# Staging of weight combinations in the unused triangle of P^T, and a late first layer on four accumulators, in a kernel of attention and two matrix products on one core

## The chip, the cores and the metric

The kernel runs on one core of a Trainium2 chip. The metric is the device time of one execution in microseconds (us). The engines are named as in the profile: PE is TensorE (matrix products), DVE is VectorE, ACT is ScalarE, POOL is GpSimd and SP is SyncE, whose queue issues the transfers (DMA).

## What is computed

A forgetting attention (4 batches, 8 heads, 576 positions, 64 columns each), then one layer with mish between two matrix products, then a gated layer. All is float32.

```
scores = scale * q @ k^T + (cum[:, None] - cum[None, :])      # cum: running sum of log f
attn   = softmax(where(causal, -1e9, scores))
x = (attn @ v) as 2304 x 512
h = x @ w_in                                # 512 -> 2048, the "first layer"
x = (h * tanh(softplus(h))) @ w_out         # mish, 2048 -> 512
a, b = x @ w1, x @ w2                       # 512 -> 1024 each
out = ((a * b) @ w3) @ w_out2               # 1024 -> 1024 -> 512
```

## The kernel before

A float32 product is made of three products of halves: an operand is split into hi (a cast on ACT) and lo (the raw value less hi, on DVE or POOL), and hi·hi, hi·lo and lo·hi are added up in the accumulator. The large layers are moreover made as products of 2 x 2 blocks with seven products for eight; the operands of the seven are sums of blocks, on the weights' side made once beforehand.

**Phase A** takes 85 slots with PE's order written out. It computes the attention of 16 pairs of heads. P is the softmax's numerator, which PE transposes block by block; ACT and DVE copy the blocks into `pt`, a tile with four chunks of 128 keys for each of two pairs and two heads. Since attention is causal, the chunks 2 and 3 of the columns 0 to 255 are never written. As filler between the attention's steps run the conversions of the weights, the product w3 @ w_out2 (`wp`), the first layer of batches 0 to 2 (`l1_unit`), and `build`, which makes the combinations of weights: `put` casts one into a tile `bs` (three buffers; ACT), subtracts for its lo half (POOL) and stores both to the scratch `ws` in HBM (SP), 84 times 256 KB. The sums for it are made by POOL in the one tile `bt`.

**Phase B** begins with the late first layer: batch 3, 32 units (16 rows of blocks `m`, two halves of tokens) of 12 matmuls each, in the accumulators `ps_y` and `ps_z` by turns. Each unit ends with a copy to one of three tiles `h` (ACT) and a store to the scratch `h_scr` (SP). Beside it the 16 tiles `y` of the first two batches are loaded from `h_scr` (576 KB each) and put through mish on ACT. Two quads follow, each a g layer (`k_layer` with n = 8: seven products in the order 1, 2, 6, 5, 7, 3, 4, each with eight values of f, 12 matmuls for each f), an m layer (operands T from `m_operands`) and an h layer (`k_layer` with n = 4).

`operand` makes one operand for product o and f: for product 2 it makes two sums in place in y (DVE; they are for the later products), for product 6 two others, and `halves` makes hi and lo. Operands live in a pool of 12 `x` tiles, which also holds the eight tiles X of batch 3 during the late first layer. PE's order is the program's; the other engines' orders come from a scheduler that plans by its own model, and each engine takes its instructions strictly in that order.

## Time and profile before

| what | us |
|---|---|
| median of three runs | 1038.78 |
| the three runs | 1034.14, 1038.78, 1043.15 |
| profiled execution, its own time | 1039.57 |
| its span | 1037.8 |
| TensorE busy in it | 920.5 |

The span is that of the instructions on the core, and the profiled execution's own time is 1.8 us longer. Times of the trace count from the start of the span. The granted clock is a share of TensorE's full speed, 2.4 GHz; 0.50 is 1.2 GHz. PE starts the late first layer at 470.97 and the first g layer at 537.54.

### The profile page before, as it was taken

To read this page: it belongs to the slowest core of one execution; us is meant where nothing else is said; L and a number is where in the kernel's file an instruction comes from. 1 tells how busy PE (TensorE), PEld (TensorE's weight loads), DVE (VectorE), ACT (ScalarE), POOL (GpSimd) and SP (SyncE) were. 2 spreads that over 40 slices of the span, in tenths; PEclk is the share of its full clock that TensorE was granted. 3 is DMA by queue.
4 is the path that set the end of the run, shared out by engine and by line. 5 is a ranking of instruction groups with operands and counts; after the bars stand their busy time and mean duration, and the time that the engine had idled before them with its cause. 6 is when DMAs were issued, how large, how long until landed. Compare 5 with 4: busy or idle time off the path is not lost.

```text
span 1037.8 us, 17939 instructions
## 1 busy us (share of the span) xinstructions
PE 920.5 (89%) x6432; PEld 835.9 (81%) x6432; DVE 575.5 (55%) x985; ACT 507.1 (49%) x1123; POOL 469.5 (45%) x435
## 2 busy tenths in 40 slices
PE   0589998889888999995998897999999889899998
PEld 0466667768767788884998896999999889899998
DVE  6966666654545456631038639665458833644462
ACT  1665565666656565538233444644474254422143
POOL 4633344675656640011034669645176466611053
PEclk9999999999999999998999898999999889999999
DMA  6455556787778887659724462864987435455551
GB/s 181 149 169 165 156 172 199 235 286 253 248 264 270 290 282 218 216 191 414 231 96 126 120 198 95 281 223 167 353 301 221 126 120 166 136 163 164 165 182 70
DMA packets 133071, 209.10 MB, mean 201 GB/s; under 512 B 12053, under 2 KB 66725, under 8 KB 132981
## 3 DMA queue, kind: packets, MB, share of 16 engines
q1 hardware_dynamic: 132980, 207.95, 61.6%
q8 instruction: 51, 0.84, 0.3%
q14 instruction: 40, 0.32, 0.1%
HBM read 140.86 MB, written 66.95 MB: 200 GB/s over the span
## 4 chain that ended last, share of the span: by engine, by line
PE 45%; DVE 12%; DMA 9%; issue 3%; POOL 3%; ACT 2%; SPq 1%; ACTq 0%; DVEq 0%; POOLq 0%
PE ps_x L961 9%; PE ps_x L889 8%; PE ps_y L889 5%; PE ps_z L889 5%; PE ps_z L961 4%; PE ps_l L513 4%; DMA ws<-bs 3%; DMA h_scr<-h 3%; PE ps_y L961 2%; DVE y L855 2%; PE ps_z L513 2%; PE ps_y L513 2%; DVE g_l L870 2%; DVE g_r L860 2%; DMA y<-h_scr 2%
## 5 line engine op out<-in xcount | busy, mean ns | idle before, releaser
L513 PE MATMUL ps_l<-x,wi 128*128 128x288 f32 x1152 | 171.5, 303 | 5.2 <-ACT h L517 5.1
L513 PEld LDWEIGHTS ps_l<-x,wi 128*128 128x128 f32 x1152 | 157.6, 190 | 17.0 <-ACT h L517 7.7
L870 POOL TENSOR_TENSOR g_l<-y,g_h 128x576 fp32r<-128x576 f32 x66 | 106.6, 1626 | 123.8 <-ACT g_h L868 104.3
L870 POOL TENSOR_TENSOR h_l<-ab,h_h 128x576 fp32r<-128x576 f32 x34 | 51.2, 1520 | 122.0 <-ACT h_h L868 116.5
L371 ACT ACTIVATE P<-P,sum 128x128 f32<-128x128 f32 (+2 forms) x144 | 83.1, 578 | 32.5 <-DVE sum L361 21.6
L868 ACT CAST g_h<-y 128x576 fp32r<-128x576 f32 x96 | 63.8, 673 | 66.3 <-PE ps_z L889 35.1
L889 PE MATMUL ps_x<-g_h,ws 128*128 128x288 f32 x512 | 95.5, 308 | 0.3 <-ACT o L919 0.3
L870 DVE TENSOR_TENSOR g_l<-y,g_h 128x576 fp32r<-128x576 f32 x30 | 34.3, 1143 | 102.5 <-ACT g_h L868 102.4
L889 PEld LDWEIGHTS ps_x<-g_h,ws 128*128 128x128 f32 x512 | 80.7, 200 | 0.8 <-ACT o L919 0.5
L889 PE MATMUL ps_x<-g_l,ws 128*128 128x288 f32 x256 | 59.4, 315 | 18.5 <-POOL g_l L870 14.7
L361 DVE CUSTOM_DVE_ANT_0 P<-ps_s,m 128x128 f32<-128x128 f32 (+3 forms) x128 | 56.5, 484 | 23.4 <-PE ps_s L340 22.1
L409 PE MATMUL ps_t<-ident,P 128*128 128x128 f32 x320 | 51.9, 298 | 19.5 <-ACT pt L424 10.6
L409 PEld LDWEIGHTS ps_t<-ident,P 128*128 128x128 f32 x320 | 40.1, 152 | 29.6 <-ACT P L371 13.9
L111 POOL TENSOR_TENSOR x<-xx,x 128x288 fp32r<-128x288 f32 x32 | 26.9, 862 | 81.6 <-ACT x L97 69.6
L889 PEld LDWEIGHTS ps_x<-g_l,ws 128*128 128x128 f32 x256 | 43.7, 201 | 21.3 <-POOL g_l L870 16.5
L340 PE MATMUL ps_s<-aug 64*128 64x128 f32 (+3 forms) x128 | 36.5, 554 | 23.2 <-POOL wo L111 23.1
L961 PE MATMUL ps_x<-T,gs 128*128 128x288 f32 x384 | 54.7, 297 | 2.2 <-DVE C L976 1.4
L340 PE MATMUL ps_s<-raw 64*128 64x128 f32 (+3 forms) x256 | 49.9, 470 | 6.3 <-DMA raw<-in_qk_dram 5.7
L788 POOL TENSOR_TENSOR bs<-bt,bs 128x256 fp32r<-128x256 f32 x48 | 39.1, 815 | 35.6 <-ACT bs L787 35.4
L961 PE MATMUL ps_x<-T,ws 128*128 128x288 f32 x384 | 54.2, 296 | 0.8 <-DVE C L976 0.8
L961 PEld LDWEIGHTS ps_x<-T,gs 128*128 128x128 f32 x384 | 52.2, 189 | 3.1 <-DVE C L976 1.9
L517 ACT COPY h<-ps_l 128x288 f32<-128x288 f32 x96 | 37.4, 392 | 32.7 <-PE ps_l L513 18.2
(211 smaller groups left out, 2255.6 us busy)
## 6 DMA issues: line engine op xcount, KB each, us to landing
ws<-ws SPq DMA_DIRECT2D x112, 512.0 KB
ws<-bs SPq DMA_DIRECT2D x84, 256.0 KB
h_scr<-h SPq DMA_DIRECT2D x128, 144.0 KB
y<-h_scr SPq DMA_DIRECT2D x32, 576.0 KB
ws<-gs SPq DMA_DIRECT2D x56, 256.0 KB
raw<-in_qk_dram SPq DMA_DIRECT2D x32, 288.0 KB
cvrt<-in_w3t_dram SPq DMA_DIRECT2D x16, 512.0 KB
cvri<-in_w_in_dram SPq DMA_DIRECT2D x16, 512.0 KB
```

What stands on the lines that cost most here:

```text
L111: ins = self.nc.gpsimd.tensor_tensor(lo[..., c], raw[..., c], f32(hi[..., c]), ALU.subtract)
L340: mm(ps[:, 512 * hh:512 * hh + n], t[r, q0:q0 + 128], t[r, 0:n], start=first, stop=not first)
L361: ttr(P[hh][:, :n], ps[:, 512 * hh:512 * hh + n], self.m1[:, 512 - n:], -0.125, 3.0e38, ALU.add, ALU.min, st[hh])
L371: ins = nc.scalar.activation(t[:, :n], t[:, :n], AF.Exp, bias=b, scale=-1.0, accum_out=self.sums[:, i:i + 1])
L409: tr(self.ps_t[hh][:, o + 128 * k:o + 128 * k + 128], P[:, 128 * k:128 * k + 128], self.ident)
L513: mm(o[:, :TB], w, x, start=i == 0, stop=i == 11)
L517: self.nc.scalar.copy(t, o[:, :TB])
L788: pool.tensor_tensor(st[:, 256:], x, f32(st[:, :256]), ALU.subtract)
L868: self.nc.scalar.copy(hi, raw)
L870: eng.tensor_tensor(lo, raw, f32(hi), ALU.subtract)
L889: mm(ps[:, r, :TB], w[:, 256 * a + 128 * e:256 * a + 128 * e + 128], ops[i][b][:, r], start=o in (1, 5, 2) and f == 0 and (a, b) == (0, 0) ...
L961: mm(bank[:, r, :TB], w[:, 256 * a + 128 * k:256 * a + 128 * k + 128], T[o, k][:, b, r], start=o in (1, 2, 5) and (k, a, b) == (0, 0, 0), ...
```

## The change

Three things are changed. `put` numbers its calls, and four of seven go into the unused triangle of `pt` (in place g of 0 to 3), the other three into `bs`. The late first layer takes four accumulators in turn, its copies are made by DVE, and its units come in the order of halves: all 16 blocks m of half 0, then those of half 1. In the k layers the operands are made four steps ahead where it was three, the two sums of product 2 stand behind `halves`, and the lo part is DVE's for each odd k (k is the number of the step in its layer) where it was DVE's for each third; the same rule goes for the T tiles.

```diff
@@ -60,7 +60,7 @@
 ORDER_K = (1, 2, 6, 5, 7, 3, 4)
 ORDER_M = (1, 5, 6, 2, 3, 7, 4)
 AHEAD = 7
-T_AHEAD = 3
+T_AHEAD = 4
 
 
 def f32(ap):
@@ -88,6 +88,7 @@
         self.V = {}
         self.filler = deque()
         self.nl1 = 0
+        self.late_l1 = False
         self.pe = None
 
 
@@ -158,7 +159,7 @@
 
     def l1_bank(self):
         self.nl1 += 1
-        return self.ps_l[self.nl1 % 2]
+        return self.ps_l[self.nl1 % len(self.ps_l)]
 
 
     def pools(self):
@@ -514,7 +515,10 @@
             if i == 11:
                 t = self.base.tile([128, TB], F32, name=f"h{b}_{m}_{half}", tag="h", bufs=HB)
                 with self.tc.high_priority(offset=HP_L1):
-                    self.nc.scalar.copy(t, o[:, :TB])
+                    if self.late_l1:
+                        self.nc.vector.tensor_copy(t, o[:, :TB])
+                    else:
+                        self.nc.scalar.copy(t, o[:, :TB])
                 self.nc.sync.dma_start(self.h_scr[128 * m:128 * m + 128, b * S + TB * half:b * S + TB * half + TB], t)
 
         i = 0
@@ -565,6 +569,7 @@
     def phase_a(self):
         nc = self.nc
         self.X, self.wo2t, self.w3s, self.wi, self.parts = {}, [], {}, {}, {}
+        self.nbs = 0
         self.att_pool()
 
         first = []
@@ -717,7 +722,8 @@
         self.late = ctx.enter_context(tc.tile_pool(name="late", bufs=1))
         p = ctx.enter_context(tc.tile_pool(name="psb", bufs=1, space=PSUM))
         self.banks = [p.tile([128, 1024], F32, name=n) for n in ("ps_x0", "ps_x1", "ps_y", "ps_z")]
-        self.ps_l = [t[:, :512] for t in self.banks[2:]]
+        self.ps_l = [t[:, :512] for t in (self.banks[2], self.banks[3], self.banks[0], self.banks[1])]
+        self.late_l1 = True
         self.bk = [t.rearrange("p (r w) -> p r w", r=2) for t in self.banks]
         self.wq, self.wcur = deque(), deque()
         self.wsrc = deque((l, t) for q in range(2) for l, n in enumerate((28, 28, 14)) for t in range(n) if q or l != 1)
@@ -783,10 +789,16 @@
         a11, a12, a21, a22 = self.quarters_of(l, *r)
 
         def put(o, x):
-            st = self.att.tile([128, 512], F32R, name=f"bs{l}_{u}_{o}", tag="bs", bufs=3)
-            nc.scalar.copy(st[:, :256], x)
-            pool.tensor_tensor(st[:, 256:], x, f32(st[:, :256]), ALU.subtract)
-            nc.sync.dma_start(self.ws[l][self.place(l, u, o)], f32(st))
+            self.nbs += 1
+            g = self.nbs % 7
+            if g < 4:
+                st = self.pt[:, g, 2:4, 0:256].bitcast(F32R)
+            else:
+                st = self.att.tile([128, 512], F32R, name=f"bs{l}_{u}_{o}", tag="bs", bufs=3)
+                st = st.rearrange("p (h w) -> p h w", h=2)
+            nc.scalar.copy(st[:, 0], x)
+            pool.tensor_tensor(st[:, 1], x, f32(st[:, 0]), ALU.subtract)
+            nc.sync.dma_start(self.ws[l][self.place(l, u, o)].rearrange("p (h w) -> p h w", h=2), f32(st))
 
         if k == 0:
             put(1, a11)
@@ -851,9 +863,6 @@
         b11, b12, b21, b22 = b
         tt = self.nc.vector.tensor_tensor
         hi, lo = [self.x_tile(f"{name}_{x}").rearrange("p (r w) -> p r w", r=2) for x in "hl"]
-        if o == 2:
-            tt(b11, b12, b11, ALU.subtract)
-            tt(b12, b22, b12, ALU.subtract)
         raw = {1: b11, 2: b21, 3: b22, 4: b21, 5: b11, 7: b12}.get(o)
         if o == 6:
             raw = self.x_tile(f"{name}_r", F32).rearrange("p (r w) -> p r w", r=2)
@@ -862,11 +871,14 @@
             tt(b21, b21, raw, ALU.subtract)
             return hi, lo
         self.halves(raw, hi, lo, k)
+        if o == 2:
+            tt(b11, b12, b11, ALU.subtract)
+            tt(b12, b22, b12, ALU.subtract)
         return hi, lo
 
     def halves(self, raw, hi, lo, k):
         self.nc.scalar.copy(hi, raw)
-        eng = self.nc.vector if k % 3 == 2 else self.nc.gpsimd
+        eng = self.nc.vector if k % 2 else self.nc.gpsimd
         eng.tensor_tensor(lo, raw, f32(hi), ALU.subtract)
 
     def k_layer(self, name, n, src, c, hook):
@@ -985,7 +997,7 @@
     def phase_b(self):
         self.late_pool()
         self.y = {}
-        l1 = list(self.filler) + [x for m in range(16) for half in range(2) for x in self.l1_unit(B - 1, m, half)]
+        l1 = list(self.filler) + [x for half in range(2) for m in range(16) for x in self.l1_unit(B - 1, m, half)]
         self.gate = {}
         n = -(-len(l1) // 192) * 12
 
```

The orders show where the scheduler has put this. In ACT's order before, in the late first layer, the copies of the units (h_m_half) stand among the mishes (the ACTIVATEs on y):

```order
L517 COPY h_1_0_4857<-ps_z 128x288
L842 ACTIVATE y_7_5041<-y_7_5041 128x1152
L842 ACTIVATE y_8_5074<-y_8_5074 128x1152
L842 ACTIVATE y_9_5107<-y_9_5107 128x1152
L842 ACTIVATE y_10_5140<-y_10_5140 128x1152
L842 ACTIVATE y_11_5173<-y_11_5173 128x1152
L842 ACTIVATE y_12_5206<-y_12_5206 128x1152
L842 ACTIVATE y_13_5239<-y_13_5239 128x1152
L517 COPY h_1_1_4872<-ps_y 128x288
L842 ACTIVATE y_14_5272<-y_14_5272 128x1152
L842 ACTIVATE y_15_5305<-y_15_5305 128x1152
L517 COPY h_2_0_4890<-ps_z 128x288
```

After, ACT has only mishes there, and DVE has the copies. In its order halfway through the late first layer, the lo part of g_1_3 (product 1, f = 3) and four sums on y stand between the copies of the first units of half 1:

```order
L519 COPY h_15_0_5022<-ps_y 128x288
L882 TENSOR_TENSOR g_1_3_l<-y_3_4861,g_1_3_h 128x576
L875 TENSOR_TENSOR y_2_4828<-y_2_4828 128x2x288
L875 TENSOR_TENSOR y_3_4861<-y_3_4861 128x2x288
L519 COPY h_0_1_5040<-ps_z 128x288
L876 TENSOR_TENSOR y_2_4828<-y_10_5092,y_2_4828 128x2x288
L876 TENSOR_TENSOR y_3_4861<-y_11_5125,y_3_4861 128x2x288
L519 COPY h_1_1_5055<-ps_x_4756 128x288
L519 COPY h_2_1_5073<-ps_x_4757 128x288
```

So these five operations are ahead of the g layer now, and the copies of units 16 (h_0_1) and 17 wait behind some of them. The second place is the end of product 1 in the second g layer, DVE's order before (names are layer g, product, f, and h, l or r for hi, lo and raw):

```order
L855 TENSOR_TENSOR y_3_6978<-y_3_6978 128x2x288
L870 TENSOR_TENSOR g_1_5_l<-y_5_7544,g_1_5_h 128x576
L856 TENSOR_TENSOR y_3_6978<-y_11_7677,y_3_6978 128x2x288
L855 TENSOR_TENSOR y_4_7522<-y_4_7522 128x2x288
L855 TENSOR_TENSOR y_5_7544<-y_5_7544 128x2x288
L856 TENSOR_TENSOR y_4_7522<-y_12_7698,y_4_7522 128x2x288
L856 TENSOR_TENSOR y_5_7544<-y_13_7717,y_5_7544 128x2x288
L855 TENSOR_TENSOR y_6_7582<-y_6_7582 128x2x288
L855 TENSOR_TENSOR y_7_7592<-y_7_7592 128x2x288
L870 TENSOR_TENSOR g_2_0_l<-y_8_7616,g_2_0_h 128x576
L856 TENSOR_TENSOR y_6_7582<-y_14_7752,y_6_7582 128x2x288
L856 TENSOR_TENSOR y_7_7592<-y_15_7759,y_7_7592 128x2x288
```

There g_2_0_l stands as the last but two. And after, from the sums on y_6 on:

```order
L875 TENSOR_TENSOR y_6_7541<-y_6_7541 128x2x288
L882 TENSOR_TENSOR g_1_7_l<-y_7_7551,g_1_7_h 128x576
L876 TENSOR_TENSOR y_6_7541<-y_14_7708,y_6_7541 128x2x288
L875 TENSOR_TENSOR y_7_7551<-y_7_7551 128x2x288
L882 TENSOR_TENSOR g_2_1_l<-y_9_7591,g_2_1_h 128x576
L876 TENSOR_TENSOR y_7_7551<-y_15_7715,y_7_7551 128x2x288
L882 TENSOR_TENSOR g_2_3_l<-y_11_7633,g_2_3_h 128x576
L882 TENSOR_TENSOR g_2_5_l<-y_13_7673,g_2_5_h 128x576
L882 TENSOR_TENSOR g_2_7_l<-y_15_7715,g_2_7_h 128x576
```

The first lo of product 2 that DVE makes was that of f = 0 behind all but two of the sums; now it is that of f = 1, and those of f = 0, 2, 4 and 6 are POOL's.

## Rows read from the trace of the kernel before

**Rows 1.** The page, part 1, TensorE: busy time, share of the span, instructions.
```profile
PE 920.5 (89%) x6432; PEld 835.9 (81%) x6432; DVE 575.5 (55%) x985; ACT 507.1 (49%) x1123; POOL 469.5 (45%) x435
```

**Rows 2.** Windows: width, busy us by engine (instructions), clock, DMA share, GB/s.
```profile
186.00:386.00 200.00, 177.43 (x1245) 147.37 (x1244) 107.47 (x261) 120.77 (x363) 127.92 (x159) 0.95 0.82 269
537.00:569.00 32.00, 28.29 (x202) 28.05 (x201) 28.29 (x26) 11.88 (x20) 18.27 (x11) 0.95 0.41 125
569.00:589.00 20.00, 16.23 (x101) 15.50 (x100) 16.53 (x14) 8.47 (x14) 14.47 (x9) 0.85 0.36 105
627.00:652.00 25.00, 17.41 (x104) 16.03 (x103) 23.48 (x16) 12.23 (x21) 25.00 (x15) 0.80 0.31 107
784.00:822.00 38.00, 33.91 (x237) 33.45 (x236) 33.60 (x31) 14.66 (x23) 21.02 (x13) 0.91 0.56 164
879.00:898.00 19.00, 15.44 (x106) 15.20 (x105) 15.23 (x13) 9.00 (x15) 15.70 (x9) 0.91 0.39 128
```

**Rows 3.** Waits by line in 185 to 385: in total, times, longest.
```profile
POOL bs L788 <- ACT bs L787: 51.9, 48, 3.3
ACT bs L787 <- DMA ws<-bs: 29.9, 29, 3.6
...
ACT bs L787 <- POOL bt L795: 5.4, 5, 1.7
```

**Rows 4.** Timeline of ScalarE: start, length; idle before and its releaser.
```profile
271.49 0.40 ACT L787 CAST bs<-cvu 128x256 fp32r<-128x256 f32 x1 [3.60 <-DMA ws<-bs]
```

**Rows 5.** Timeline of TensorE in the staging, the same columns.
```profile
272.55 1.54 PE L409 MATMUL ps_t<-ident,P 128*128 128x128 f32 x6 [2.47 <-ACT P L371]
```

**Rows 6.** Timeline of TensorE, late first layer.
```profile
470.97 1.88 PE L513 MATMUL ps_z<-x,wi 128*128 128x288 f32 x12 [2.00 <-ACT h L517]
...
490.17 3.25 PE L513 MATMUL ps_y<-x,wi 128*128 128x288 f32 x12 [8.64 <-ACT h L517]
...
535.95 1.75 PE L513 MATMUL ps_y<-x,wi 128*128 128x288 f32 x12
537.54 0.42 PE L889 MATMUL ps_x<-g_h,ws 128*128 128x288 f32 x2
```

**Rows 7.** Timeline of ScalarE, late first layer.
```profile
479.22 0.38 ACT L517 COPY h<-ps_z 128x288 f32<-128x288 f32 x1
...
489.74 0.38 ACT L517 COPY h<-ps_y 128x288 f32<-128x288 f32 x1
...
493.60 0.40 ACT L517 COPY h<-ps_z 128x288 f32<-128x288 f32 x1 [0.60 <-DMA h_scr<-h]
```

**Rows 8.** Timeline of SyncE's queue, late first layer.
```profile
478.62 0.32 SPq L518 DMA_DIRECT2D h_scr<-h  x1
```

**Rows 9.** A window of the late first layer, columns as in rows 2.
```profile
484.00:488.00 4.00, 0.00 (x0) 0.00 (x0) 0.66 (x1) 3.47 (x3) 0.00 (x0) 0.50 1.02 413
```

**Rows 10.** Timeline of TensorE, stops at products 2, 4 and 2.
```profile
554.46 0.53 PE L889 MATMUL ps_y<-g_l,ws 128*128 128x288 f32 x2 [3.71 <-DVE g_l L870]
...
647.33 0.85 PE L889 MATMUL ps_x<-g_l,ws 128*128 128x288 f32 x2 [3.64 <-POOL g_l L870]
...
806.75 0.85 PE L889 MATMUL ps_y<-g_l,ws 128*128 128x288 f32 x2 [3.80 <-DVE g_l L870]
```

**Rows 11.** Timeline of VectorE, beside product 1 of both g layers.
```profile
548.58 0.74 DVE L856 TENSOR_TENSOR y<-y,y 128x576 f32<-128x576 f32 x1
549.25 0.74 DVE L855 TENSOR_TENSOR y<-y 128x576 f32<-128x576 f32 x1
...
784.19 1.97 DVE L855 TENSOR_TENSOR y<-y 128x576 f32<-128x576 f32 x1 [0.45 <-POOL g_l L870]
...
804.75 1.95 DVE L870 TENSOR_TENSOR g_l<-y,g_h 128x576 fp32r<-128x576 f32 x1
```

**Rows 12.** Timeline of GpSimd in the first g layer.
```profile
536.50 7.72 POOL L870 TENSOR_TENSOR g_l<-y,g_h 128x576 fp32r<-128x576 f32 x4 [61.37 <-ACT g_h L868]
...
595.81 1.44 POOL L870 TENSOR_TENSOR g_l<-y,g_h 128x576 fp32r<-128x576 f32 x1 [1.77 <-ACT g_h L868]
```

## The prediction

> **What bounds the kernel now.** I read the page first, then the kernel in windows, then in the lossy windows the gaps of TensorE and the queue that ends each. TensorE is busy for 920.5 us, 89% of the span [rows 1], so only what it does not lose can be won: idle time, and time at a low clock. I count the loss of a stretch as idle plus busy × (1 − granted clock). Each row of [rows 2] gives one: 200 − 177.4 + 177.4 × 0.05 = 31.4 us in the staging stretch of phase A (186 to 386); 3.7 + 1.4 = 5.1 in products 1 and 2 of the first g layer (537 to 569), 4.1 + 3.1 = 7.1 in those of the second (784 to 822); 3.8 + 2.4 = 6.2 in product 6 (569 to 589); 7.6 + 3.5 = 11.1 in the last product, 4, of the first g layer (627 to 652) and 3.6 + 1.4 = 5.0 in that of the second (879 to 898). The late first layer is the other one. Its last unit takes 537.54 − 535.95 = 1.59, so 32 units need 50.9; they take 537.54 − 470.97 = 66.6 [rows 6], a loss of 15.7. The change aims at all of these and at no other place, so the sum is made of them.
>
> **1. Staging in P^T.** What now stands last: ACT's cast into a `bs` tile waited 29 times, 29.9 us in all, for the store of the tile's former content, and POOL's subtraction 51.9 us for ACT's cast; 5.4 us more of ACT are for POOL's `bt` [rows 3]. ACT takes its work in order, so what is queued behind the cast waits too: at 271.49 a cast came after 3.60 us of waiting for a store [rows 4]; the exponentials of P stood behind it, and TensorE, which transposes P, was idle for 2.47 us until 272.55 [rows 5]. Seven places instead of three let seven combinations be under way; the wait for a store then begins only when the seventh before it has not landed. Price: the same casts, subtractions and bytes, since the places in P^T are ones that the causal triangle never fills. What may eat it: a store now has 1 KB pieces where it had 2 KB, and the DMA engines are at a share of 0.82 there [rows 2]; and `bt` is one tile, so POOL's chain through it stays. The bounds: nothing, if the stores are limited by what the DMA engines move; and 18, which is the gaps of TensorE that I can follow to a store (about 10 of the 22.6 idle us) and all but one of the 8.9 us of clock. I take 8, nearer the lower end, since the next wait in the same queue (POOL's `bt`, ACT's other casts) is right behind. **−8 (0 to −18).**
>
> **2. The late first layer.** What it removes: ACT's copy of a finished unit stood among the 16 mishes, each of which waits for its load of y. After the copy at 479.22 the next ran at 489.74 with seven mishes between, and a later one at 493.60 waited for a store of h [rows 7]. TensorE had two accumulators, stood still for 8.64 us until 490.17 [rows 6], and was granted 0.50, which is 1.2 GHz, in 484 to 488 [rows 9]. Now VectorE copies, which has little else there, and four accumulators are in turn. But the copy writes one of three h buffers, and these are freed by stores. The DMA engines are full until the y loads are through (share 1.02 in [rows 9]). The first of those stores was issued at 478.62 [rows 8] and had let nobody go by 488. With it one place earlier in SP's queue I let it land near 487. So three units are copied, four more fill the accumulators, and the eighth unit starts at about 487.9 where now the sixth starts at 490.17. From there 25 units × 1.59 = 39.7 give 527.6; the next store holds the ninth for some 3 us, and the half clock after the stop costs some 2.5: 533.3 instead of 537.54. **−4.2.** Bounds: 0, if the stores land as before and the two units gained before the stop are lost at it in waits for stores; −8, if the stop is short enough for the clock not to fall. The first gap of 2.00 at 470.97 [rows 6] stays: the banks are those of phase A and its last copy is ACT's.
>
> What else moves there: with the units in the order of halves the four X tiles of half 0 are free halfway, so g_1_2, g_1_3 and the y sums of f = 2 and 3 are done beside it. They stand in VectorE's queue before h_0_1's copy, and wait for ACT's and POOL's part: at most some 4.5 us (a cast, a subtraction of 1.9, five operations of 0.7). Four accumulators last 4 × 1.59 = 6.4, so TensorE doesn't feel it. The loads of ws also go later, behind units 16 to 23, and still end some 15 us before product 1.
>
> **3. Products 1 and 2 of a g layer.** VectorE makes 16 sums for later products and a part of the lo's; the lo's of product 2 stood behind all of it. TensorE's stops in front of product 2, 3.71 and 3.80 us, end with VectorE's g_l [rows 10]. What an operation costs there depends on POOL: VectorE's 128x576 takes 0.74 alone, one every 0.67 (548.58, 549.25), and 1.95 beside POOL [rows 11]; POOL's takes 1.44 alone, and four beside VectorE took 7.72, or 1.93 each [rows 12]. So a pair takes 1.93; VectorE's share of it is its pitch of 0.67, POOL's the rest, 1.26. The check: from 784.19 to 806.70 VectorE did 17 operations [rows 11], and POOL about 9 in the same time: 17 × 0.67 + 9 × 1.26 = 22.7, measured 22.5. Now the first lo of product 2 on VectorE is the 20th operation there, with 5 to 6 of POOL beside it (half the lo's where it had two thirds): 20 × 0.67 + 5.5 × 1.26 = 20.3, so it ends at 804.2 from 783.9. Product 1 ends as before at 802.5, f = 0 of product 2 (POOL's) takes 1.6, f = 1 is wanted at 804.2 too: **−6.5 of the 7.1** in the second g layer. In the first, 10 operations are left there at the end of the late first layer, with 4 of POOL's: 6.7 + 5.0 = 11.7 to 13.5, and wanted after 12.8 + 1.6 = 14.4: the stop goes with its clock, **−5.1**. Operands four steps ahead change little by themselves: ACT's casts already run ahead as far as the x buffers let them.
>
> **4. Products 6 and 4.** Product 6 has two VectorE sums and a lo for each f, and three of the lo's were VectorE's: 19 × 0.67 + 5 × 1.26 = 19.0, which is what it took (8 × 1.6 = 12.8 and the 6.2 of loss). Now four are: 20 × 0.67 + 4 × 1.26 = 18.4, so −0.6, and some of the first lies a step earlier beside product 2: **−1 each, −2** (0 to −6). At product 4 POOL is the last: it worked 25.00 of 25.00 us [rows 2], with T's and gate pieces, and TensorE waited 3.64 us for its g_l [rows 10]. Two of its eight lo's and two T's go to VectorE, but VectorE was itself busy 23.5 of 25: **−2** in the first g layer (−1 to −4) and **−0.5** in the second.
>
> **Sum.** 8 + 4.2 + 6.5 + 5.1 + 2 + 2.5 = 28.3. The profiled execution is 1039.57 us, 0.8 above the median of 1038.78: 1039.6 − 28.3 = **1011 us**, the median likewise 1010.5.
>
> **The rivals.**
> (a) The h buffers, not the accumulators, hold the late first layer: stores land as late as now, and the units gained are given back: 1011 + 4 = 1015. For it: the copy at 493.60 waited for a store [rows 7]. Chance 0.10.
> (b) VectorE and POOL don't overlap at all: an operation holds the other for its whole length, so 20 × 0.74 + 5.5 × 1.44 = 22.7, product 2 of the second g layer waits 2.4 us again and its clock falls: 1011 + 6.5 = 1017.5. Against it: a pair measured 1.93, not 0.74 + 1.44 = 2.18, and 17 × 0.74 + 9 × 1.44 = 25.5 where 22.5 were measured. Chance 0.10. The Trainium skill's page "SBUF — State Buffer", section "SBUF: two separate sides", says this: the pair of ports that VectorE and GpSimd share is an exclusive lock, held for the whole instruction, and the loser blocks fully. By that rule the second g layer would gain next to nothing here; the trace agrees that the two hold each other up, and not in the amount.
> (c) The staging brings nothing, since the stores or `bt` take the place of the freed tile: 1011 + 8 = 1019. For it: POOL waits more for ACT's cast than ACT for stores, and the DMA share is 0.82. Chance 0.14.
> (d) More goes than I count: with four steps ahead the small stops of products 6 and 4 vanish and their low clock with them (6 + 4 more): about 1001. Chance 0.08.
> (e) The other side: VectorE becomes the bound. If an operation of VectorE costs 1.9 whenever POOL has any work, and POOL has work as long as before, then the four lo's more of VectorE in products 2, 6 and 4 add 4 × 1.9 = 7.6 a layer, 15 in two, and the 16 of parts 3 and 4 are not won: 1011 + 16 + 15 = 1042, or about 1050 where the clock falls at these stops as it does now (0.80 in [rows 2]). It decides where POOL's shorter share doesn't shorten the time that VectorE spends beside it. Against it: VectorE at 0.74 alone is half of POOL's 1.44, so work moved to it makes the sum of both smaller. Chance 0.05.
> (f) The change doesn't do what it says: the places in P^T wait for the readers of P^T and the operands stand a step ahead only in name, and the time is 1035 to 1040. Chance 0.03.
>
> **How the numbers follow.** The forecast, 1011, has 0.50. Rivals (a), (b) and (c) lie within 8 us of it and exclude one another not at all; all three together would be 1030. The range goes from (d)'s 1001, with part 1's upper bound of 10 more weighed in at less than half, to the three together: 997 to 1029. A change of under 1% (1028.4 to 1049.2) can hardly be told from none, as the three runs before differ by 0.9%. Faster by more than that: 0.50 + 0.10 + 0.10 + 0.14 + 0.08, less 0.06 for combinations: 0.86. Same: 0.10, the combinations, (f) and a part of (e). Slower: 0.04.
>
> **What would show it.** Part 1: waits of ACT's staging casts for stores well under 30 us, idle time of TensorE in 186 to 386 at 15 or less, and the late first layer starting some 8 us earlier. Part 2: one stop of 4 to 6 us in it, later, ended by VectorE's copy that waits for a store of h; 62 us instead of 66.6. Part 3: no stop over 1 us at product 2, clock 1.00 through it. Part 4: the same stops in product 6, a little shorter. I am wrong if the stops in front of product 2 are still there, if the waits for stores only turn into waits for `bt`, or if VectorE's operations take 1.9 all through.

## The result, and the profile after

The changed kernel takes 1002.0 us (median of four executions, 1000.61 to 1007.84), the kernel before 1036.63 in the same comparison; the ratio is 0.967 with an interval of 0.961 to 0.973. That is 34.6 us less, where 28 were forecast. The profiled execution of the changed kernel is the fastest of its four (1000.61, span 998.8); that of the kernel before (1039.57) was a further one, longer than three of the four that the median is from. So the two profiles stand 39.0 apart, 4 more than the medians. I account for these 39.0, by the starts of the stages in TensorE's timeline. The first stage ends where the last four matmuls of the first pair's attention with v (those on `vb`) begin, 2.6 us after the first of them; the experiments call this moment the first product of attention with v.

| stage | before | after | change | forecast |
|---|---|---|---|---|
| start to the end of the first product of attention with v | 79.98 | 77.14 | −2.8 | 0 |
| from there to the end of phase A | 390.99 | 383.27 | −7.7 | −8 |
| late first layer | 66.57 | 60.42 | −6.2 | −4.2 |
| first g layer, products 1 and 2 | 31.05 | 25.59 | −5.5 | −5.1 |
| second g layer, products 1 and 2 | 32.35 | 27.19 | −5.2 | −6.5 |
| product 6 and product 5 behind it, both g layers | 65.47 | 62.56 | −2.9 | −2 |
| product 4, first g layer | 24.24 | 19.44 | −4.8 | −2 |
| product 4, second g layer | 17.90 | 14.42 | −3.5 | −0.5 |
| all else up to TensorE's end (m layers, h layers, products 7 and 3) | 325.45 | 325.01 | −0.4 | 0 |

The page's first part, TensorE's row, answers to [rows 1]:

```profile
PE 900.3 (90%) x6432; PEld 818.9 (82%) x6432; DVE 608.5 (61%) x1051; ACT 492.3 (49%) x1091; POOL 412.6 (41%) x401
```

TensorE has 20 us less of busy time with the same instructions, since it ran less at a low clock; the rest of the 39 was idle time. The windows of the same stages, as in [rows 2], with product 6 of both g layers:

```profile
176.00:376.00 200.00, 178.81 (x1299) 149.29 (x1298) 114.04 (x277) 124.91 (x380) 130.15 (x161) 0.98 0.87 276
520.80:553.00 32.20, 32.20 (x244) 32.20 (x243) 29.04 (x31) 13.03 (x20) 15.15 (x10) 1.00 0.50 159
546.00:567.00 21.00, 17.34 (x124) 16.31 (x123) 19.24 (x18) 9.86 (x16) 11.71 (x8) 1.00 0.41 130
602.00:622.00 20.00, 15.25 (x102) 14.79 (x101) 19.93 (x18) 10.04 (x18) 15.93 (x10) 0.91 0.32 104
759.00:787.00 28.00, 26.55 (x201) 26.08 (x200) 26.97 (x29) 11.91 (x19) 13.56 (x8) 1.00 0.62 182
787.00:806.00 19.00, 14.88 (x96) 13.86 (x95) 17.84 (x17) 7.08 (x12) 9.84 (x6) 0.91 0.36 113
844.00:859.00 15.00, 13.54 (x102) 13.31 (x101) 13.61 (x14) 7.92 (x14) 9.15 (x6) 1.00 0.44 153
```

By the same count (idle plus busy × (1 − clock)) the staging loses 21.2 + 3.6 = 24.8 us of 200 where it lost 31.4. Products 1 and 2 of the first g layer lose nothing, with the clock at 1.00 all through; those of the second lose 1.5 (7.1 before). Product 6 loses 3.7 in the first (546 to 567; 6.2 before), product 4 there 6.1 (11.1 before) and 1.5 in the second (844 to 859; 5.0 before). In product 4 of the first g layer GpSimd is busy for 15.9 of 20 us and no longer all the time; VectorE is now, 19.9 of 20.

The whole staging stretch, from the end of the first row of the table to the end of phase A, before and after (the same columns):

```profile
79.98:470.97 390.99, 356.77 (x2493) 291.49 (x2487) 220.70 (x548) 230.12 (x667) 176.83 (x214) 0.97 0.73 232
77.14:460.41 383.27, 349.68 (x2494) 286.65 (x2488) 221.19 (x548) 227.89 (x667) 176.80 (x214) 0.99 0.76 237
```

TensorE's idle time hardly fell, from 34.2 to 33.6 us; the gain is in its busy time, 7.1 us less for the same products at a higher granted clock. In the window of 200 us the idle time is 21.2 after 22.6, where the prediction had named 15 or less as a sign.

The waits of the staging, by line (in total, times, longest), answer to [rows 3]; the staging casts into P^T are named `pt`:

```profile
POOL pt L800 <- ACT pt L799: 34.9, 21, 5.3
...
POOL bs L800 <- ACT bs L799: 10.4, 18, 1.7
...
ACT bs L799 <- POOL bt L813: 8.3, 8, 2.1
...
ACT pt L799 <- POOL bt L807: 6.3, 3, 3.3
...
ACT bs L799 <- POOL bt L811: 6.1, 5, 1.6
ACT pt L799 <- POOL bt L805: 6.0, 4, 1.8
...
ACT pt L799 <- DMA ws<-pt: 0.9, 1, 0.9
```

The waits of the casts for stores, 29.9 us before, are down to 0.9. GpSimd waits for the casts for 45 us in sum where it waited 52. The casts' waits for `bt` grew: 26.7 us in these four lines, where the four of the kernel before have 15.9 (5.4, 5.1, 2.9 and 2.5). So of the 29 us won at the stores some 11 came back as waits for `bt`. TensorE's longest stop left in the staging ends with an exponential that had waited for VectorE, and not for a store:

```profile
328.91 0.77 ACT L372 ACTIVATE P<-P,sum 128x576 f32<-128x576 f32 x1 [0.91 <-DVE sum L369]
...
329.83 0.66 PE L414 MATMUL ps_t<-ident,P 128*128 128x128 f32 x4 [2.93 <-ACT P L372]
```

TensorE's timeline in the late first layer answers to [rows 6]:

```profile
460.41 2.82 PE L514 MATMUL ps_z<-x,wi 128*128 128x288 f32 x12 [2.34 <-ACT h L521]
...
469.96 3.34 PE L514 MATMUL ps_x<-x,wi 128*128 128x288 f32 x24
478.09 3.25 PE L514 MATMUL ps_y<-x,wi 128*128 128x288 f32 x12 [4.79 <-DVE h L519]
482.62 1.88 PE L514 MATMUL ps_z<-x,wi 128*128 128x288 f32 x12 [1.28 <-DVE h L519]
...
520.83 0.43 PE L901 MATMUL ps_x<-g_h,ws 128*128 128x288 f32 x2
```

Seven units run before the stop: one at 460.41, two at 463.02, one each at 466.79 and 468.38, and the two at 469.96. The eighth waits 4.79 us, the ninth 1.28. VectorE's timeline says what for (these are the copies, with the idle time before and its releaser):

```profile
467.69 0.46 DVE L519 COPY h<-ps_x 128x288 f32<-128x288 f32 x1 [1.82 <-DMA h_scr<-h]
...
477.57 0.46 DVE L519 COPY h<-ps_y 128x288 f32<-128x288 f32 x1 [3.85 <-DMA h_scr<-h]
482.10 0.46 DVE L519 COPY h<-ps_z 128x288 f32<-128x288 f32 x1 [4.07 <-DMA h_scr<-h]
```

Each of the three copies waited for a store of h out of the buffer that it writes. The windows of 4 us, as in [rows 9], show that the clock fell after the stop, and for one window only (another low one, 0.71 at 462 to 466, lies behind the layer's first gap of 2.34):

```profile
474.00:478.00 4.00, 0.00 (x0) 0.00 (x0) 0.42 (x1) 3.26 (x3) 0.00 (x0) 1.00 1.04 422
478.00:482.00 4.00, 3.25 (x12) 2.90 (x12) 0.03 (x1) 2.96 (x4) 0.00 (x0) 0.57 0.78 302
482.00:486.00 4.00, 3.38 (x25) 3.38 (x26) 2.16 (x5) 0.76 (x1) 0.00 (x0) 1.00 0.37 131
```

The stops that are left in the g layers, in TensorE's timeline, answer to [rows 10]. The first two lie in product 6 and the third in product 4 of the first g layer, the last in product 1 of the second:

```profile
559.32 0.53 PE L901 MATMUL ps_x<-g_l,ws 128*128 128x288 f32 x2 [1.41 <-POOL g_l L882]
...
561.82 0.53 PE L901 MATMUL ps_x<-g_l,ws 128*128 128x288 f32 x2 [1.44 <-DVE g_l L882]
...
618.28 0.85 PE L901 MATMUL ps_x<-g_l,ws 128*128 128x288 f32 x2 [3.70 <-DVE g_l L882]
...
772.06 0.53 PE L901 MATMUL ps_x<-g_l,ws 128*128 128x288 f32 x2 [1.21 <-DVE g_l L882]
```

### The profile page after: what moved, and what is told of

It is laid out like the page before. It is cut to its first block, busy times and chain, and to the rows that moved or that the text cites. A ratio compares the mean times of both kernels' runs of the same rounds, so it can differ in the third digit from the quotient of the medians.

```text
span 998.8 us, 17936 instructions
## 1 busy us (share of the span) xinstructions
PE 900.3 (90%) x6432; PEld 818.9 (82%) x6432; DVE 608.5 (61%) x1051; ACT 492.3 (49%) x1091; POOL 412.6 (41%) x401
## 4 chain that ended last, share of the span: by engine, by line
PE 59%; DVE 16%; DMA 11%; ACT 6%; issue 4%; POOL 3%; SPq 1%; ACTq 0%; DVEq 0%; POOLq 0%
PE ps_x L901 11%; PE ps_x L973 10%; PE ps_l L514 8%; PE ps_z L901 5%; PE ps_y L901 5%; PE ps_z L973 5%; PE ps_s L443 3%; PE ps_y L973 2%; ACT P L372 2%; PE ps_s L341 2%; DMA cvru<-in_w_out_dram 2%; PE ps_x L514 2%; DMA cvri<-in_w_in_dram 2%; PE ps_t L410 2%; DMA y<-h_scr 2%
## 5 line engine op out<-in xcount | busy, mean ns | idle before, releaser
L882 POOL TENSOR_TENSOR g_l<-y,g_h 128x576 fp32r<-128x576 f32 x48 | 74.3, 1552 | 130.5 <-PE ps_y L514 56.7
L901 PE MATMUL ps_x<-g_h,ws 128*128 128x288 f32 x512 | 93.2, 301 | 2.9 <-ACT g_h L880 2.6
L882 POOL TENSOR_TENSOR h_l<-ab,h_h 128x576 fp32r<-128x576 f32 x24 | 35.5, 1480 | 126.1 <-ACT h_h L880 115.1
L901 PEld LDWEIGHTS ps_x<-g_h,ws 128*128 128x128 f32 x512 | 77.7, 193 | 4.0 <-ACT g_h L880 3.3
L882 DVE TENSOR_TENSOR g_l<-y,g_h 128x576 fp32r<-128x576 f32 x48 | 53.7, 1121 | 44.7 <-ACT g_h L880 44.1
L901 PE MATMUL ps_x<-g_l,ws 128*128 128x288 f32 x256 | 56.8, 304 | 11.1 <-DVE g_l L882 8.3
L410 PE MATMUL ps_t<-ident,P 128*128 128x128 f32 x320 | 46.7, 280 | 10.3 <-ACT pt L425 6.6
L973 PEld LDWEIGHTS ps_x<-T,ws 128*128 128x128 f32 x384 | 52.1, 189 | 2.9 <-ACT x L931 1.7
L521 ACT COPY h<-ps_l 128x288 f32<-128x288 f32 x96 | 37.5, 390 | 33.2 <-PE ps_l L514 17.3
L410 PEld LDWEIGHTS ps_t<-ident,P 128*128 128x128 f32 x320 | 37.0, 142 | 18.7 <-ACT pt L425 9.7
```

The lines of the kernel that those rows point to most:

```text
L410: tr(self.ps_t[hh][:, o + 128 * k:o + 128 * k + 128], P[:, 128 * k:128 * k + 128], self.ident)
L521: self.nc.scalar.copy(t, o[:, :TB])
L882: eng.tensor_tensor(lo, raw, f32(hi), ALU.subtract)
L901: mm(ps[:, r, :TB], w[:, 256 * a + 128 * e:256 * a + 128 * e + 128], ops[i][b][:, r], start=o in (1, 5, 2) and f == 0 and (a, b) == (0, 0) ...
L973: mm(bank[:, r, :TB], w[:, 256 * a + 128 * k:256 * a + 128 * k + 128], T[o, k][:, b, r], start=o in (1, 2, 5) and (k, a, b) == (0, 0, 0), ...
```

## The experiments

Stage times are read as in the table above, from one trace of each kernel. "Staging" is the stretch in the table's second row. Kernels 5, 6, 8, 9 and 10 were executed once, so that their medians are single times without an interval. The spread between traces is to be kept in mind: the late first layer of the change took 60.4 to 62.6 us in the six kernels that have its edits as they are (changed, 2, 5, 6, 7, 10), and the staging of the change 379.9 to 387.8 in ten.

| kernel | staging | late first layer | g1st: 1+2 | 6 | 4 | g2nd: 1+2 | 6 | 4 | median us |
|---|---|---|---|---|---|---|---|---|---|
| before | 391.0 | 66.6 | 31.1 | 19.2 | 24.2 | 32.4 | 19.0 | 17.9 | 1036.6 |
| changed | 383.3 | 60.4 | 25.6 | 17.6 | 19.4 | 27.2 | 19.4 | 14.4 | 1002.0 |
| 1 staging alone | 384.1 | 68.2 | 31.1 | 18.9 | 24.2 | 31.7 | 19.0 | 17.9 | 1028.7 |
| 2 late first layer alone | 393.3 | 62.6 | 25.6 | 18.9 | 24.1 | 31.7 | 17.1 | 17.4 | 1023.6 |
| 3 operands alone | 392.8 | 66.9 | 26.9 | 19.3 | 19.6 | 27.6 | 19.1 | 14.4 | 1019.0 |
| 4 four h buffers | 387.8 | 58.4 | 25.6 | 19.4 | 19.9 | 27.6 | 17.6 | 14.4 | 1001.9 |
| 5 third lo | 381.7 | 62.0 | 25.6 | 17.2 | 21.8 | 31.7 | 17.1 | 14.4 | 1010.2 |
| 6 three ahead | 385.7 | 61.7 | 25.6 | 17.6 | 21.5 | 27.6 | 19.4 | 15.1 | 1007.6 |
| 7 all lo on VectorE | 386.1 | 62.1 | 25.6 | 14.5 | 16.9 | 26.1 | 14.5 | 12.8 | 994.7 |
| 8 copies by ScalarE | 383.3 | 61.2 | 25.6 | 18.9 | 19.5 | 27.2 | 19.4 | 14.4 | 1004.5 |
| 9 two accumulators | 382.8 | 65.2 | 25.6 | 19.4 | 19.9 | 27.5 | 17.6 | 14.4 | 1006.0 |
| 10 four places | 390.7 | 62.4 | 25.6 | 17.6 | 19.9 | 27.6 | 19.4 | 14.4 | 1014.0 |
| 11 = 4 and 7 | 379.9 | 58.6 | 25.6 | 14.5 | 17.1 | 26.1 | 14.5 | 12.8 | 989.3 |
| 12 = 11, T shared | 383.4 | 58.0 | 25.6 | 15.0 | 16.3 | 26.1 | 15.0 | 14.0 | 990.7 |

**My theory** was that the change is three independent ones, each in its own stage, with the prices of the prediction. The rivals were its (a) to (e). The first three runs take the parts one by one.

**1. The staging alone.** Only `put` and its counter are taken from the change:

```diff
+            self.nbs += 1
+            g = self.nbs % 7
+            if g < 4:
+                st = self.pt[:, g, 2:4, 0:256].bitcast(F32R)
...
```

> Only the first part of the change: four of seven staging places in the unused triangle of P^T. My theory (the three parts act in separate stages and add up): phase A ends 8 us earlier (462 to 464 instead of 470.97, less or more by what the start of the execution differs), with the waits of the staging casts for stores under 10 us; the late first layer stays at 66 to 67 us and the g layers at 113.8 and 108.4; 1029 us. Rival (the staging brings nothing, the gain at the end of phase A comes from elsewhere): phase A ends at 469 to 472, 1037 us.

Phase A ended at 462.60, and the time is 1028.7 (ratio 0.992, 0.989 to 0.995). The casts' waits for stores, two lines of the waits:

```profile
ACT pt L794 <- DMA ws<-pt: 1.0, 1, 1.0
...
ACT bs L794 <- DMA ws<-pt: 0.4, 1, 0.4
```

1.4 us together. The late first layer took 68.2, and the g layers moved by 0.6 at most. The theory holds in time, and rival (c), that the staging brings nothing, falls.

**2. The late first layer alone.** Four accumulators, copies by VectorE, the order of halves:

```diff
...
-        self.ps_l = [t[:, :512] for t in self.banks[2:]]
+        self.ps_l = [t[:, :512] for t in (self.banks[2], self.banks[3], self.banks[0], self.banks[1])]
...
-        l1 = list(self.filler) + [x for m in range(16) for half in range(2) for x in self.l1_unit(B - 1, m, half)]
+        l1 = list(self.filler) + [x for half in range(2) for m in range(16) for x in self.l1_unit(B - 1, m, half)]
```

> Only the second part: late first layer on four accumulators, copies by VectorE, units in the order of halves. My theory: phase A as before (470 to 472), the late first layer 60 to 61 us instead of 66.6, the first g layer shorter by up to 2 (the operations that are done beside the late first layer), the second g layer at 108.4 as before; 1030 us. Rival (the h buffers hold the layer and the gain of 6 us needs the earlier y loads of the other parts): 65 to 67 us, 1036 us.

62.6 us for the late first layer, between theory and rival but nearer the theory; 1023.6 (0.988, 0.983 to 0.993). TensorE's start of it and its stop:

```profile
471.32 1.88 PE L514 MATMUL ps_z<-x,wi 128*128 128x288 f32 x12 [2.15 <-ACT h L521]
...
489.13 3.25 PE L514 MATMUL ps_y<-x,wi 128*128 128x288 f32 x12 [6.41 <-DVE h L519]
```

What I did not expect: the stop at product 2 of the first g layer is gone, all 5.5 us, with none of the third part. VectorE does a lo and four sums more during the late first layer there, and GpSimd a lo, which the order of halves allows; I take them for the reason.

**3. The operands alone.**

```diff
-T_AHEAD = 3
+T_AHEAD = 4
-        eng = self.nc.vector if k % 3 == 2 else self.nc.gpsimd
+        eng = self.nc.vector if k % 2 else self.nc.gpsimd
```

and the two sums of product 2 behind `halves`.

> Only the third part: operands four steps ahead, the sums of product 2 behind the halves, every second lo on VectorE. My theory: phase A and the late first layer as before; second g layer 99 to 100 us instead of 108.4, of which the stop at product 2 is 5 to 6.5 and product 4 3 to 4; the first g layer 103 to 106 instead of 113.8, since it starts without the operations that the second part lets run beside the late first layer; 1020 us. Rival (VectorE and GpSimd exclude each other wholly, and the first g layer's gain comes from the second part alone): the first g layer at 109 or more.

1019.0 (0.985, 0.981 to 0.990): the first g layer 104.2, the second 99.5, both in the theory's bounds and not at the rival's 109. Products 1 and 2 of the first g layer went from 31.1 to 26.9 by this part alone. The three parts alone gained 7.5, 12.6 and 17.3 us, 37.3 in sum, and together 34.6. By the stages, parts 2 and 3 remove the same stop there (4.2 us are counted twice); the medians by themselves are too wide to show it.

**4. Four h buffers** in the changed kernel (`HB = 3` becomes `HB = 4`).

> The changed kernel with four h buffers where it has three. My theory (behind the accumulators the h buffers hold the late first layer: VectorE's copies wait for stores of h): the stops of 4.79 and 1.28 us in the late first layer shrink by one unit's worth, and it takes 57 to 59 us instead of 60.4; nothing else moves; 999 us. Rival (the y loads fill the DMA engines, and the store lands when it lands; a fourth buffer only moves the stop by one unit): still 60 to 61.

58.4 us for the late first layer, so the h buffers do hold it behind the accumulators. The stops are smaller, and the longer one is still a copy that waits for a store:

```profile
480.68 1.85 PE L514 MATMUL ps_z<-x,wi 128*128 128x288 f32 x12 [0.88 <-DVE h L519]
485.30 2.04 PE L514 MATMUL ps_x<-x,wi 128*128 128x288 f32 x8 [2.77 <-DVE h L519]
```

The median, 1001.9 (0.964, 0.960 to 0.969), can't be told from the changed kernel's, and the 999 of the expectation were not reached: 2 us are lost in the spread, the staging took 387.8 here and product 6 of the first g layer 19.4.

**5. Every third lo on VectorE**, as before, in the changed kernel (`k % 2` becomes `k % 3 == 2`).

> The changed kernel with the lo of each third step on VectorE as before, and all else of the change. My theory (product 4 was won by the moved lo's of g and T, since GpSimd was full there): product 4 goes back to 22 to 24 us in the first g layer and 16 to 18 in the second; product 2 of the second g layer keeps 12.8, or loses up to 2 again. Rival (the fourth step ahead won product 4): it stays at 19.4 and 14.4.

Product 2 of the second g layer stopped again for the full 3.79 us:

```profile
782.81 0.77 PE L901 MATMUL ps_y<-g_l,ws 128*128 128x288 f32 x2 [3.79 <-DVE g_l L882]
```

so the stop there is removed by the moved lo's: the rest of the change, which this kernel has, leaves it whole. I had expected 2 us at most. Product 4 of the first g layer gave back 2.4 of 4.8 (21.8, just under the theory's bounds), that of the second nothing: its 14.4 is the rival's number.

**6. Operands three steps ahead** in the changed kernel (`T_AHEAD = 3`).

> The changed kernel with operands three steps ahead. My theory (the casts run ahead as far as the buffers let them anyway): all products within 0.7 us of the changed kernel, product 4 at 19.4 and 14.4. Rival (the step ahead won product 4 or product 2): one of them loses 3 us or more again.

Product 4 of the first g layer gave back 2.1 of 4.8, that of the second 0.7. So my sentence that the step ahead changes little by itself was wrong for product 4: there it is about as much as the moved lo's.

**7. Every lo on VectorE**, in the changed kernel:

```diff
-        eng = self.nc.vector if k % 2 else self.nc.gpsimd
+        eng = self.nc.vector
```

> The changed kernel with every lo on VectorE, none on GpSimd. My theory (beside a GpSimd operation VectorE loses 1.26 us, an operation of its own costs 0.67): product 6 takes 24 x 0.67 = 16.1 us in both g layers instead of 17.6 and 19.4, products 1 and 2 together (16 sums and 16 lo's, 21.4 us) show no stop, product 4 gets shorter since GpSimd has only the gate pieces: 17 to 19 and 13 to 14; 995 to 997 us. Rival (VectorE becomes the bound, an operation costs 1.9 as long as GpSimd has any work): product 6 at 19 or more, new stops in products 1 and 2, 1010 us.

994.7 us (0.958, 0.954 to 0.963), a little better than expected. Product 6 takes 14.5 in both layers, product 4 takes 16.9 and 12.8, and products 1 and 2 of the second g layer 26.1. VectorE's timeline in product 6 shows its three operations for each f, none stretched:

```profile
558.94 0.76 DVE L882 TENSOR_TENSOR g_l<-g_r,g_h 128x576 fp32r<-128x576 f32 x1
559.62 0.75 DVE L869 TENSOR_TENSOR g_r<-y,y 128x576 f32<-128x576 f32 x1
560.40 0.76 DVE L871 TENSOR_TENSOR y<-y,g_r 128x576 f32<-128x576 f32 x1
561.18 0.76 DVE L882 TENSOR_TENSOR g_l<-g_r,g_h 128x576 fp32r<-128x576 f32 x1
```

This decides against rival (e): VectorE has more to do and is done sooner, since what it does is not stretched to 1.9 any more. GpSimd's help there was worth less than what it cost VectorE. A part was given back: the first m layer took 95.3 us here and 92.6 in the changed kernel.

**8. Copies by ScalarE** into the four accumulators.

```diff
-                    if self.late_l1:
-                        self.nc.vector.tensor_copy(t, o[:, :TB])
-                    else:
-                        self.nc.scalar.copy(t, o[:, :TB])
+                    self.nc.scalar.copy(t, o[:, :TB])
```

> The changed kernel with the copies of the late first layer on ScalarE, as before, into the same four accumulators and in the order of halves. My theory (the stop ends with a store of h whichever engine copies; the accumulators and not the engine gave the 6 us): 60 to 62 us for the late first layer. Rival (the copies have to leave the mishes' queue): 64 to 67.

61.2 us, with one stop of 8.30 in place of two:

```profile
481.74 1.57 PE L513 MATMUL ps_y<-x,wi 128*128 128x288 f32 x5 [8.30 <-ACT h L517]
```

ScalarE's timeline has this copy behind a mish that waited for its load, and not waiting for a store:

```profile
480.24 1.16 ACT L849 ACTIVATE y<-y 128x1152 f32<-128x1152 f32 x1 [0.22 <-DMA y<-h_scr]
481.31 0.38 ACT L517 COPY h<-ps_y 128x288 f32<-128x288 f32 x1
```

So the mishes' queue held the copy longer than the h buffers did, and the units behind it then found buffers free. The time is in my bounds, but my reason, that a store ends the stop whichever engine copies, did not hold here. Against the changed kernel that is 0.8 us, within the 60.4 to 62.6 of the stage: no gain by VectorE's copying shows.

**9. Two accumulators**, with copies by VectorE.

```diff
-        self.ps_l = [t[:, :512] for t in (self.banks[2], self.banks[3], self.banks[0], self.banks[1])]
+        self.ps_l = [t[:, :512] for t in self.banks[2:]]
```

> The changed kernel with two accumulators in the late first layer, copies on VectorE. My theory (three h buffers and two accumulators hold five units where four accumulators hold seven): the stop comes two units earlier and is 3 us longer, 63 to 65 us for the late first layer. Rival (the copy by VectorE alone gave the gain): 60 to 61.

65.2 us. The stop came after five units and was longer:

```profile
476.83 3.25 PE L514 MATMUL ps_y<-x,wi 128*128 128x288 f32 x12 [6.72 <-DVE h L519]
```

So of the 6.2 us the accumulators are worth 4.7 by these two traces, and 2.6 by the longest trace with four.

**10. Four staging places**, all in P^T (`self.nbs % 4` for `self.nbs % 7`).

> The changed kernel with four staging places, all in P^T, instead of seven: 1 KB pieces in every store. My theory (the number of places counts, the 1 KB pieces cost nothing that TensorE sees): between the kernel before and the changed one, the stretch from the first product of attention with v to the end of phase A 385 to 389 us (391.0 before, 383.3 changed), waits of the casts for stores 10 to 25 us. Rival (stores in 1 KB pieces are slower and hold the staging): 391 or more, waits over 30 us.

390.7 us in the staging stretch, as the kernel before; the waits of the staging:

```profile
POOL pt L800 <- ACT pt L799: 52.0, 48, 4.0
...
ACT pt L799 <- DMA ws<-pt: 22.4, 17, 2.4
```

My number was missed, though the 22.4 us of waits for stores are in its bounds: one place more gave nothing (against 391.0 to 393.3 in the three kernels with the old staging). Whether that is the number of places or the 1 KB pieces, which here are in every store, this run doesn't separate. What it shows is that four places with 1 KB pieces are about as fast as three with 2 KB. That the step from four places to seven is what pays is likely, since pieces of 1 KB are in four of seven stores there, but not shown.

**11. The fourth h buffer and every lo on VectorE.**

> The changed kernel with every lo on VectorE and four h buffers. My theory (the two act in separate stages): late first layer 58 to 60 us, product 6 at 14.5, product 4 at 17 and 12.8 as with every lo on VectorE alone; 990 to 994 us. Rival (without GpSimd's part VectorE's queue is late in the late first layer, and the fourth buffer's gain is lost there): 62 us for it, 994 to 997 us.

989.3 us (0.954, 0.950 to 0.957), just under the expected 990 to 994: the fastest kernel here, 1.3% below the changed one, with both stages as in the single runs.

**12. The same, but the lo's of T by turns on VectorE and GpSimd.**

> The kernel with every lo of the g and h layers on VectorE and four h buffers, but the lo's of T shared by turns between VectorE and GpSimd, as in the changed kernel. My theory (an operation of GpSimd costs VectorE 1.26 where VectorE is the last, and a full T on VectorE held the m layer of the first quad at 93.7): product 4 of the first g layer 16 to 18.5, the first m layer 92 to 92.8; 988 us, within 2 of the kernel with all on VectorE. Rival (GpSimd's T operations slow VectorE's sums in product 4 as its lo's did): product 4 of the first g layer back at 19 or more, 991 us.

990.7 us (0.955, 0.952 to 0.958), not to be told from run 11. Product 4 of the first g layer is 16.3, shorter than with all on VectorE, which speaks against the rival; but the m layer behind it took 96.6 where I expected 92 to 92.8 (93.7 in run 11), and product 4 of the second g layer 14.0. So the second half of my expectation is refuted. The trace shows what holds the m layer here: TensorE stops once for 3.52 us, for a copy of ScalarE that stands behind the cast of a T, and this cast had waited 3.60 us for a sum `r` of VectorE:

```profile
618.98 0.67 ACT L880 CAST T<-r 128x576 fp32r<-128x576 f32 x1 [3.60 <-DVE r L956]
...
620.24 2.87 PE L973 MATMUL ps_x<-T,gs 128*128 128x288 f32 x12 [3.52 <-ACT C L978]
```

VectorE came to that sum late, since the lo's of T ahead of it took 1.96 us beside GpSimd's; in run 11, whose m layer begins within 0.2 us of the same time, the lo took 0.74 and the sum ran 3.6 us earlier. VectorE's timeline in run 12:

```profile
615.78 1.96 DVE L882 TENSOR_TENSOR T<-r,T 128x576 fp32r<-128x576 f32 x1
617.67 3.14 DVE L956 TENSOR_TENSOR r<-x,r 128x576 f32<-128x576 f32 x2
```

and in run 11:

```profile
613.41 0.74 DVE L882 TENSOR_TENSOR T<-r,T 128x576 fp32r<-128x576 f32 x1
614.07 0.74 DVE L956 TENSOR_TENSOR r<-x,r 128x576 f32<-128x576 f32 x1
```

So GpSimd's operations on T do slow VectorE's sums, as the rival has it, but the price falls in the m layer and not in product 4. What holds the first m layer in runs 7 and 11 is another wait: stops of 2.03 and 1.45 us, and of 1.96, that end with VectorE's sums into C. Why these come late stays open.

## Why the prediction was right

The time, 1002.0, lies within the range and 8.5 us below the forecast of the median. It is nearer to rival (d), 1001, and half of (d) came: product 4 won more than was counted, while the stops of product 6 stayed. The terms came out as follows.

**The staging** gained 7.7 us where 8 were forecast, and run 1 gained 6.9 by it alone. The first step is the one told: the casts no longer wait for stores. The next wait in the queue, `bt`, took back 11 of the 29 us, as was feared. The size is right to some us, and that it came so near is luck: run 1's executions give 7.5 with an interval from 5 to 11, and single traces anything from 3 to 13 (379.9 to 387.8 with this staging, 391.0 to 393.3 without). The last step of the chain is not what was told: of TensorE's idle time, 10 us of which I had followed to stores, only 0.6 went, and the gain is that the clock fell less (granted 0.97 before, 0.99 after). Why it fell less with nearly as much idle time, no run shows.

**The start of phase A** gave 2.8 us that no step had. In the other runs' kernels, which have the same source there, the first product of attention with v begins anywhere between 76.2 and 79.6, in those without the staging (78.0 and 76.2) as in those with it. So I count it to the spread; whether it differs by execution or by what the scheduler makes of the first 80 us wasn't tried.

**The late first layer** gained 6.2 where 4.2 were forecast. Seven units and the store of h as the end of the stop were as told: the eighth unit started 17.7 us after the first (forecast 16.9). What was too large is the price behind it: the ninth waited 1.28 us and not 3, and only one window behind the stop ran at a low clock. (The sum itself has a slip: 527.6, 3 and 2.5 are 533.1 and not 533.3.) The trace of the changed kernel is the shortest of six here; by the others, up to 62.6, the gain is 4.0 to 6.2. Rival (a) was the wrong alternative: accumulators and h buffers add up. Two accumulators less cost 4.7 (run 9; 65.2 against at most 62.6), one h buffer more gains 2.0 (run 4; 58.0 to 58.6 in runs 4, 11 and 12), and who copies can't be told from nothing (run 8).

**Products 1 and 2.** In the first g layer 5.5 where 5.1 were forecast, in the second 5.2 where 6.5 were; there the stop moved into product 1 (1.21 us at 772.06) instead of going: it waits for g_1_7_l, a lo of product 1 behind the same sums, which the prediction had not looked at. The prices 0.67 and 1.26 hold. The first lo of product 2 on VectorE, its 20th operation there, with five of GpSimd's beside it, ends 20.0 us after the first began (754.01 to 774.01), where 20.3 were forecast and rival (b), which adds full lengths, has 22.7. The first and the 20th in VectorE's timeline:

```profile
754.01 1.11 DVE L882 TENSOR_TENSOR g_l<-y,g_h 128x576 fp32r<-128x576 f32 x1
...
773.27 0.74 DVE L882 TENSOR_TENSOR g_l<-y,g_h 128x576 fp32r<-128x576 f32 x1
```

Run 5 shows that the moved lo's decide in the second layer. Run 7's product 6, with no operation of GpSimd, is no check of the 0.67 by its time: of its 24 operations (16.1 by 0.67 each, measured 14.5) ten lie before the product begins, and in the rows shown three take 2.24. In the first layer, as run 2 shows, the same stop also goes by what the order of halves lets run early; the prediction had both in one step.

**Products 6 and 4.** The term that was mis-sized is product 4: 2.5 forecast, 8.3 measured, 4.8 and 3.5. I had taken VectorE's 23.5 busy us of 25 [rows 2] for a sign that it had no room. But these 23.5 were stretched by GpSimd's operations, as my own prices say: each lo that leaves GpSimd gives VectorE 1.26 back and takes 0.67. And I had put the step ahead at nothing, where run 6 gives it 2.1 of the 4.8 in the first g layer. In the second, runs 5 and 6 gave back nothing and 0.7 of the 3.5; what won the rest there stays open. Product 6 was forecast at −2, and the row of the table, −2.9, is right by luck. Only 1.2 of it is product 6, and 1.7 are product 5 behind it, which before ran its first part at the low clock. At a granted clock of 1.00 product 6 takes 17.1 us with three lo's on VectorE (runs 2 and 5) and 17.6 with four: the moved lo made it longer by 0.5, where the count, 19.0 to 18.4, has it shorter. That count had met the measured 19.0 with the clock's loss in it. What was won in product 6 is that the clock stayed up in the first g layer.

## What to carry to other kernels

Where two engines slow each other down, count what an operation costs the one that is last, not how long it takes on its own engine: here one of GpSimd cost VectorE more (1.26 us) than VectorE needed for it itself (0.67), and taking every lo from GpSimd made the kernel faster by another 7 us. A busy share near 1 is no proof that an engine has no room, if its operations are stretched by another. A gain that is read in one pair of traces is worth no more than the spread of that stage over all traces: the 7.7 of the staging could with other traces have been 3 or 13. A stop that several buffers share (accumulators, h tiles, staging places) is to be counted in units that are under way before it, and each kind of buffer adds its own.

## What was not expected of the hardware

Product 6 has the same two stops of 1.41 and 1.44 us in both g layers of the changed kernel, and took 17.6 us in one, with a granted clock of 1.00 in its window, and 19.4 in the other, with 0.91. Over all kernels that share the lo's of product 6 with GpSimd it took 17.1 to 17.6 or 18.9 to 19.4 and nothing between; the clock fell or didn't, for stops of nearly the same lengths. That is some 1.8 us in each g layer that no edit here controls, unless the stops get shorter, as in runs 7, 11 and 12 (0.66 us at most), where the clock stayed at 1.00 in both.
